# Additions and subtractions of two tensors from GpSimd to VectorE, clamps from VectorE to GpSimd, tail shifts to ScalarE

## Chip, cores and metric

The kernel runs on one core of a Trainium2 chip. The metric is the device time of one execution in microseconds (us). Before the change the median of 3 runs is 882.42 us (882.37 to 883.85).

## What is computed

Three layers follow one another, all in float32 (four batches of 576 tokens, 512 features):

```python
# 1. attention: 32 global queries see all keys, 512 local queries the global keys and a band of +-32
s_l = where(|i - j| <= 32, q_l @ k_l.T, -1e9);  a_l = softmax([q_l @ k_g.T, s_l]);  out = a_l @ v_all
# 2. dense MLP with a convolution over tokens as gate (w_in 512x1024, w_out 1024x512)
h = relu(x @ w_in);  conv = sum_k conv_w[k] * shift(h, k - 1);  x = (h * sigmoid(conv)) @ w_out
# 3. Fourier mixing, layer norm, dense MLP (w_ch1 512x2048, w_ch2 2048x512)
u = x + real(fft_features(fft_tokens(x)));  un = (u - mean(u)) / sqrt(var(u) + 1e-6)
out = u + relu(un @ w_ch1) @ w_ch2
```

The weights of layers 2 and 3 arrive as float64 (two 32-bit words a value), and the kernel itself makes float32 of them.

## The kernel before

**Weights.** There are 48 weight tiles of 128 x 512 values: 8 of `w_in` and 8 of `w_out` (`make_w`, L427), 16 of `w_ch1` and 16 of `w_ch2` (`make_c`, L698, and `make_cs`, L713). Each is loaded as 128 x 1024 words and goes through `unpack` and `from_f64` (L161 to L175): ScalarE takes the absolute value of the upper words, scaled by 2^16 (L163); a clamp to [2, TOP] follows (L164); the lower words are shifted right by 29 bits (the "tail shift", on VectorE in L168 or on ScalarE in L166); VectorE shifts the clamped value left by 3 and ors the tail in (L170), and then puts in the sign (L175). With `sign_act` the sign is made by ScalarE (L172) and multiplied in by GpSimd (L173) instead. `make_w` has the clamp on VectorE for `w_in` and on GpSimd for `w_out`; `make_c` and `make_cs` have it on VectorE always, the tail shift on VectorE for tiles 0 to 15 and on ScalarE for 16 to 31, and `sign_act` for every third tile (11 of 32).

**Two halves.** TensorE multiplies float32r operands in three passes (`mm3`, L144): high times high, and high times low twice. So each operand is split into a high part (ScalarE copy) and a low part, the difference of value and high part. For weights that is `put` (L201): ScalarE copy L203, GpSimd subtraction L204 (L718 and L719 in `make_cs`). `w_out` gets one step more, in `make_w`: sum and difference of its two halves (L433 on VectorE, L434 on GpSimd).

**Buffers for the unpacked value.** The `mag` tiles rotate: two of them up to tile 11 of layer 3, then three pieces of `misc`. A tile's chain holds one from L163 to the subtraction.

**Order of the work.** 32 attention steps (half a pair of heads each) run first; the first eight of them also unpack two tiles of layer 2 each. The units of layer 2 start in step 9 and run beside the rest of attention. Then come, interleaved, the end of layer 2, four Fourier transforms (`fft`, L616: sums and differences of mirrored tokens L623 to L629, two rounds of matmuls, and the results `ut` in L677 and L678), the 32 tiles of layer 3, and the first layer norm (`ln(0)`, L724). Layer 3's MLP is 8 chunks of 16 units: `c_g1` multiplies by `ch1`, L779 and L780 make relu and its low part, `c_g2` accumulates over `ch2`. Chunk 0 needs all 32 tiles; after it, `ln(c)` and L801 are the only work on GpSimd.

The queues of SP (loads) and TensorE follow the program's order throughout the attention part. All other orders are set ahead of time by a planner that simulates the engines with its own costs and takes, for each engine, the ready instruction of highest priority; on the chip each engine then works through its list in order. A change of costs or of engines thus changes the lists too. The weight loads of layer 2 are held back by the softmax of the step that asks for them (`anchor`).

The lines that matter most:

```python
(clamp or dve).tensor_scalar(mag, mag, 2.0, TOP, op0=ALU.max, op1=ALU.min)                       # L164
dve.scalar_tensor_tensor(val, val, 3, tail, op0=ALU.logical_shift_left, op1=ALU.bitwise_or)      # L170
gp.tensor_sub(t[:, 1], val, f32(t[:, 0]))                                                        # L204
```

Of the kernel before, what the change touches and what calls it, by code (L numbers as in the profile page):

```python
# [15 lines left out]
TOP = float(np.array([0x4FEFFFFF], np.uint32).view(np.float32)[0])  # L16
AF = mybir.ActivationFunctionType
ALU = mybir.AluOpType
# [4 lines left out]
S = SL + SG  # L23
# [5 lines left out]
NF = 274  # L29
# [95 lines left out]
def fused_kernel(ctx: ExitStack, tc: tile.TileContext, d, out):  # L125
    nc = tc.nc
    pe, act, dve, gp, sp = nc.tensor, nc.scalar, nc.vector, nc.gpsimd, nc.sync
# [27 lines left out]
    def f32(ap):  # L155
        return ap.bitcast(F32)
# [1 line left out]
    def bits(ap):  # L158
        return ap.bitcast(I32)

    def from_f64(raw, mag, clamp=None, tail_act=False, sign_act=False):  # L161
        head, tail = raw[:, :, 1], raw[:, :, 0]
        act.activation(mag, f32(head), AF.Abs, scale=65536.0)  # L163
        (clamp or dve).tensor_scalar(mag, mag, 2.0, TOP, op0=ALU.max, op1=ALU.min)  # L164
        if tail_act:
            act.activation(tail, tail.bitcast(U32), AF.Copy, scale=0.999 * 2.0**-29, bias=-0.499)  # L166
        else:
            dve.tensor_scalar(tail, tail, 29, None, op0=ALU.logical_shift_right)  # L168
        val = bits(mag)
        dve.scalar_tensor_tensor(val, val, 3, tail, op0=ALU.logical_shift_left, op1=ALU.bitwise_or)  # L170
        if sign_act:
            act.activation(f32(head), f32(head), AF.Sign)  # L172
            gp.tensor_mul(mag, mag, f32(head))  # L173
        else:
            dve.scalar_tensor_tensor(val, head, -(2**31), val, op0=ALU.bitwise_and, op1=ALU.bitwise_or)  # L175

    def fetch(pool, tag, src, after=None):
        t = pool.tile([128, 1024], I32, tag=tag, name="raw_" + tag)
# [13 lines left out]
    def unpack(pool, t, *how):  # L192
        if mags:
            mag = mags.pop(0)
            mags.append(mag)
        else:
            mag = pool.tile([128, 512], F32, tag="mag", name="mag", bufs=2)
        from_f64(t.rearrange("p (c b) -> p c b", b=2), mag, *how)
        return mag

    def put(pool, tag, val):  # L201
        t = pool.tile([128, 2, 512], F32R, tag=tag, name="w_" + tag)
        act.copy(t[:, 0], val)  # L203
        gp.tensor_sub(t[:, 1], val, f32(t[:, 0]))  # L204
        return t

    def rows_of(w, m):
# [19 lines left out]
    mp = left.enter_context(tc.tile_pool(name="mp", bufs=2))  # L227
# [192 lines left out]
    w_raw, w_in, w_out = {}, {}, {}  # L420
# [4 lines left out]

    @prio("w")
    def make_w(i):  # L427
        val = unpack(mp, w_raw.pop(i), gp if i >= 8 else dve)
        if i < 8:
            w_in[i] = put(wp, f"w{i}", val)  # L430
            return
        eo = mp.tile([128, 512], F32, tag="mag", name="mag", bufs=2)
        dve.tensor_add(eo[:, 0:256], val[:, 0:256], val[:, 256:512])  # L433
        gp.tensor_sub(eo[:, 256:512], val[:, 0:256], val[:, 256:512])  # L434
        w_out[i - 8] = put(wp, f"w{i}", eo)

    g_t, acc = {}, {}
# [178 lines left out]
    def fft(b):  # L616
        eo = eo_t[b]
        ff = fp.tile([128, 1024], F32, tag="v24", name="ff")
        fe = fd = ff[:, 0:2 * NF].rearrange("p (c n) -> p c n", c=2)
        fh = fp.tile([128, 4, NF], F32R, tag="v22", name="fh")  # L620
        fl = fp.tile([128, 4, NF], F32R, tag="v23", name="fl")
        rev = slice(S, S - NF, -1)
        gp.tensor_add(fe, eo[:, 0:2, 0:NF], eo[:, 0:2, rev])  # L623
        act.copy(fh[:, 0:2], fe)
        gp.tensor_sub(fl[:, 0:2], fe, f32(fh[:, 0:2]))
        gp.tensor_sub(fd, eo[:, 2:4, 0:NF], eo[:, 2:4, rev])
        dve.tensor_add(fd[0:1, 0], eo[0:1, 2, 0:NF], eo[0:1, 2, rev])
        act.copy(fh[:, 2:4], fd)
        gp.tensor_sub(fl[:, 2:4], fd, f32(fh[:, 2:4]))  # L629
        yield  # L630
        ab = fp.tile([128, 3084], F32R, tag="v29", name="ab")
        ah, al = [ab[0:92, 774 * i:774 * i + 774].rearrange("p (t k) -> p t k", t=3) for i in range(2)]
        bh, bl = [ab[0:92, 1548 + 768 * i:2316 + 768 * i].rearrange("p (t k) -> p t k", t=3) for i in range(2)]
        for t, (n0, nn) in enumerate(MT):
            ns = slice(n0, n0 + nn)
            o = fbank()[0:nn, 0:258]
            for c in range(2):
                mm3(o, fh[:, c, ns], fl[:, c, ns], c2[:, c, 0], c2[:, c, 1], c == 0, False)
            mm(o, fl[0:1, 2, ns], co, False, False)
            mm(o, fh[0:1, 2, ns], co, False, True)  # L640
            with pri("fev"):
                act.copy(ah[0:nn, t], o)
                dve.tensor_sub(al[0:nn, t], o, f32(ah[0:nn, t]))
            yield
            o = fbank()[0:nn, 0:256]
            for c in range(2):
                mm3(o, fh[:, 2 + c, ns], fl[:, 2 + c, ns], s2[:, c, 0], s2[:, c, 1], c == 0, c == 1)
            with pri("fev"):
                act.copy(bh[0:nn, t], o)
                dve.tensor_sub(bl[0:nn, t], o, f32(bh[0:nn, t]))  # L650
            yield
        if b not in u_t:
            u_t[b] = up.tile([128, 4, 546], F32, tag="u", name="u") if b else u0
        ut = u_t[b]
        back = slice(S - 1, HS, -1)
        for c in range(2):
            fs = slice(128 * c, 128 * c + 128)
            o = fbank()[:, 0:NF]
            for t, (n0, nn) in enumerate(MT):
                mm3(o, ah[0:nn, t, fs], al[0:nn, t, fs], c1[0:nn, t, 0], c1[0:nn, t, 1], t == 0, t == 2)  # L660
            e = eo[:, c]
            with pri("fev"):
                dve.scalar_tensor_tensor(
                    e[:, 0:HS + 1], e[:, 0:HS + 1], 0.5, o[:, 0:HS + 1], op0=ALU.mult, op1=ALU.add
                )
                dve.scalar_tensor_tensor(e[:, back], e[:, back], 0.5, o[:, 1:HS], op0=ALU.mult, op1=ALU.add)
            yield
            o = fbank()[:, 0:NF]
            for t, (n0, nn) in enumerate(MT):
                mm3(o, bh[0:nn, t, fs], bl[0:nn, t, fs], s1[0:nn, t, 0], s1[0:nn, t, 1], t == 0, t == 2)  # L670
            q = eo[:, 2 + c]
            with pri("fev"):
                dve.scalar_tensor_tensor(
                    q[:, 0:HS + 1], q[:, 0:HS + 1], 0.5, o[:, 0:HS + 1], op0=ALU.mult, op1=ALU.subtract
                )
                dve.scalar_tensor_tensor(q[:, back], q[:, back], 0.5, o[:, 1:HS], op0=ALU.mult, op1=ALU.add)
            dve.tensor_add(ut[:, c, 0:S], e[:, 0:S], q[:, 0:S])  # L677
            gp.tensor_sub(ut[:, 2 + c, 0:S], e[:, 0:S], q[:, 0:S])  # L678
            yield
        o = fbank()[0:1, 0:NF]  # L680
        for t, (n0, nn) in enumerate(MT):
            mm3(o, ah[0:nn, t, 256:257], al[0:nn, t, 256:257], c1[0:nn, t, 0], c1[0:nn, t, 1], t == 0, t == 2)
        r = ut[0:1, 2]
        dve.tensor_add(r[:, 0:HS + 1], r[:, 0:HS + 1], o[:, 0:HS + 1])
        dve.tensor_add(r[:, back], r[:, back], o[:, 1:HS])
        yield
# [3 lines left out]
    def c_slot(i):  # L690
        return (wp, f"w{i}") if i < 16 else (lw if i < 20 else fp, f"v{i}")
# [4 lines left out]

    @prio("cv")
    def make_c(i):  # L698
        t = put(*c_slot(i), unpack(mp, w_raw.pop(i), dve, i > 15, i % 3 == 0))
        if i < 16:  # L700
            ch1[i] = t
        else:
            ch2[i - 16] = t
# [8 lines left out]
    @prio("cv")  # L712
    def make_cs(i, k):  # L713
        raw = w_raw.pop(i)
        vals = [unpack(mp, raw[:, j], dve, True, (i + j) % 3 == 0) for j in range(k)]
        t = fp.tile([128, k, 2, 512], F32R, tag=f"v{i}", name="ws")
        for j in range(k):
            act.copy(t[:, j, 0], vals[j])  # L718
            gp.tensor_sub(t[:, j, 1], vals[j], f32(t[:, j, 0]))  # L719
            ch2[i + j - 16] = t[:, j]  # L720

    ln_t, dead = {}, {}
# [1 line left out]
    def ln(c):  # L724
        b, half = divmod(c, 2)
        ut = u_t[b][:, :, HS * half:HS * half + HS]
        scr = dead[min(c, 1)].rearrange("p a c -> p (a c)")
        cf = scr[:, 0:4 * HS].rearrange("p (a c) -> p a c", a=4)
        s4 = scr[:, 4 * HS:6 * HS].rearrange("p (a c) -> p a c", a=2)
        chl = xp.tile([128, 2, 4, HS], F32R, tag="xh", name="chl")  # L730
        ch, cl = chl[:, 0], chl[:, 1]
        sr = hdt[:, 3]
        gp.tensor_add(s4, ut[:, 0:2], ut[:, 2:4])
        gp.tensor_add(s4[:, 0], s4[:, 0], s4[:, 1])
        act.copy(sr[:, 0], s4[:, 0])
        dve.tensor_sub(sr[:, 1], s4[:, 0], f32(sr[:, 0]))  # L736
        yield
# [3 lines left out]
        mm(mu, ones, sr[:, 0], False, True)  # L741
        dve.tensor_sub(cf, ut, mu[:, None, :].to_broadcast([128, 4, HS]))  # L742
        act.copy(ch, cf)
        gp.tensor_sub(cl, cf, f32(ch))
        ln_t[c] = (ch, cl)
        yield
        act.activation(cf, cf, AF.Square)
        yield
        gp.tensor_add(s4, cf[:, 0:2], cf[:, 2:4])
        gp.tensor_add(s4[:, 0], s4[:, 0], s4[:, 1])  # L750
        yield
        act.copy(sr[:, 0], s4[:, 0])
        dve.tensor_sub(sr[:, 1], s4[:, 0], f32(sr[:, 0]))
# [172 lines left out]
```

## Time and profile before

| | |
|---|---|
| median of 3 runs | 882.42 us |
| the profiled execution | 884.08 us, of it span 881.9 us |
| TensorE matmul busy | 803.3 us (91%) |
| VectorE (DVE) busy | 505.4 us (57%) |
| ScalarE (ACT) busy | 347.4 us (39%) |
| GpSimd (POOL) busy | 308.6 us (35%) |
| mean granted TensorE clock | 0.94 of full speed |
| DMA | 48.33 MB, mean 55 GB/s |

Shares over the whole span say little here, as the stages differ. The span falls into: attention with the unpacking of layer 2's tiles (0 to 110 us), attention beside layer 2 (110 to 330), the change from layer 2 to layer 3 with transforms, tiles and first layer norm (330 to 550), and the MLP of layer 3 (550 to the end). Times in the trace are us from the span's start.

### The profile page before, as it was taken

How to read it: one execution, taken by the hardware profiler on the slowest of the kernel's cores; microseconds unless marked ns; L12 is line 12 of the kernel's file. 1: busy time of each engine (PE TensorE's matmuls, PEld its weight loads, DVE VectorE, ACT ScalarE, POOL GpSimd, SP SyncE). 2: the span in 40 equal slices, each digit the busy share in tenths (PEclk: the TensorE clock that was granted, in tenths of full speed). 3: DMA queues.
4: the chain of work that ended last, by engine and by line, in shares of the span. 5: the costliest groups of instructions: out<-in, count | busy, mean ns of one | idle time of the engine just before them, and what ended most of it. 6: DMA issues, size and time to landing. Idle time of an engine off the chain costs nothing. (4 is left out here: it accounts for less than half of the span.)

```text
span 881.9 us, 16202 instructions
## 1 busy us (share of the span) xinstructions
PE 803.3 (91%) x6436; PEld 752.0 (85%) x6436; DVE 505.4 (57%) x1222; ACT 347.4 (39%) x884; POOL 308.6 (35%) x318
## 2 busy tenths in 40 slices
PE   5767999999999999987779489999999999999997
PEld 3445788999899899877678388999999999999997
DVE  5786977686778767899788973221222222222212
ACT  4555555555555534555446552112121212121110
POOL 4878622132222222564676656022130404030100
PEclk8776999999999999989779699999999999999999
DMA  9460111101010012253304300000000000000000
GB/s 315 139 205 15 72 34 53 60 29 58 30 59 29 2 40 66 72 165 99 143 0 159 129 1 26 1 26 1 14 14 1 26 1 27 1 26 1 27 1 25
DMA packets 25387, 48.33 MB, mean 55 GB/s; under 512 B 1960, under 2 KB 18728, under 8 KB 25312
## 3 DMA queue, kind: packets, MB, share of 16 engines
q1 hardware_dynamic: 24480, 44.66, 15.0%
q0 software_dynamic: 832, 2.65, 1.2%
q8 instruction: 50, 0.82, 0.4%
q14 instruction: 25, 0.20, 0.1%
HBM read 43.23 MB, written 4.46 MB: 54 GB/s over the span
## 5 line engine op out<-in xcount | busy, mean ns | idle before, releaser
L302 POOL TENSOR_SCALAR pb<-pb,sm 128x224 f32<-128x224 f32 x128 | 72.9, 585 | 153.0 <-DVE sm L297 107.0
L142 PE MATMUL ps_a<-hdt,w_v 128*128 128x272 f32 x864 | 122.1, 290 | 0.0
L142 PE MATMUL ps_a<-g,w_w 128*128 128x272 f32 x768 | 114.1, 295 | 6.2 <-ACT g L486 4.4
L142 PE MATMUL ps_g<-xh,w_w 128*128 128x274 f32 x512 | 115.0, 303 | 0.0
L142 PEld LDWEIGHTS ps_a<-hdt,w_v 128*128 128x128 f32 x864 | 114.6, 191 | 0.0
L142 PE MATMUL ps_pv<-chl,w_w 128*128 128x272 f32 x768 | 109.7, 291 | 4.0 <-DVE hdt L780 3.8
L142 PE MATMUL ps_g<-chl,w_w 128*128 128x272 f32 x768 | 109.1, 290 | 2.4 <-DVE hdt L780 2.4
L142 PEld LDWEIGHTS ps_a<-g,w_w 128*128 128x128 f32 x768 | 103.2, 192 | 8.0 <-ACT g L486 5.2
L142 PEld LDWEIGHTS ps_pv<-chl,w_w 128*128 128x128 f32 x768 | 102.1, 191 | 5.3 <-issue 4.1
L142 PEld LDWEIGHTS ps_g<-chl,w_w 128*128 128x128 f32 x768 | 101.8, 190 | 3.1 <-DVE hdt L780 3.1
L780 DVE SCALAR_TENSOR_TENSOR hdt<-ps_pv,hdt 128x272 fp32r<-128x272 f32 x64 | 28.2, 440 | 122.0 <-ACT hdt L779 121.9
L142 PE MATMUL ps_a<-hdt,ws 128*128 128x272 f32 x672 | 92.5, 287 | 1.7 <-POOL ws L719 1.7
L801 POOL TENSOR_TENSOR misc<-misc,u 128x272 f32<-128x272 f32 x28 | 19.3, 720 | 212.6 <-DVE misc L800 212.6
L142 PEld LDWEIGHTS ps_g<-xh,w_w 128*128 128x128 f32 x512 | 86.7, 193 | 7.7 <-issue 4.4
L780 DVE SCALAR_TENSOR_TENSOR hdt<-ps_g,hdt 128x272 fp32r<-128x272 f32 x64 | 28.0, 437 | 109.2 <-ACT hdt L779 109.2
L142 PEld LDWEIGHTS ps_a<-hdt,ws 128*128 128x128 f32 x672 | 87.2, 188 | 1.9 <-POOL ws L719 1.9
L779 ACT ACTIVATE hdt<-ps_g 128x272 fp32r<-128x272 f32 x64 | 25.4, 397 | 128.1 <-PE ps_g L142 125.5
L779 ACT ACTIVATE hdt<-ps_pv 128x272 fp32r<-128x272 f32 x64 | 25.3, 395 | 128.0 <-PE ps_pv L142 127.1
L142 PE MATMUL ps_g<-xl,w_w 128*128 128x274 f32 x256 | 75.2, 294 | 0.0
L291 ACT ACTIVATE pb<-pb,sm 128x224 f32<-128x224 f32 x128 | 60.2, 472 | 15.6 <-DVE sm L279 15.6
L474 ACT ACTIVATE y<-y 128x272 f32<-128x272 f32 x64 | 27.5, 430 | 76.2 <-DVE y L468 76.2
L142 PE MATMUL ps_s<-qk 64*128 64x224 f32 (+1 forms) x144 | 40.1, 431 | 16.4 <-DVE smg L373 9.3
(211 smaller groups left out, 1489.4 us busy)
## 6 DMA issues: line engine op xcount, KB each, us to landing
qk<-in_qk_dram SPq DMA_DIRECT2D x16, 592.0 KB, 5.6
raw_w<-in_ch_dram SPq DMA_DIRECT2D x16, 512.0 KB, 3.8
v<-in_v_dram SPq DMA_DIRECT2D x8, 640.0 KB, 4.8
raw_v<-in_ch_dram SPq DMA_DIRECT2D x9, 512.0 KB, 5.8
out_dram<-misc SPq DMA_DIRECT2D x32, 136.0 KB, 1.8
raw_w<-in_w_in_dram SPq DMA_DIRECT2D x8, 512.0 KB, 5.1
raw_w<-in_w_out_dram SPq DMA_DIRECT2D x8, 512.0 KB, 4.0
raws<-in_ch_dram SPq DMA_DIRECT2D x7, 512.0 KB, 5.1
```

The source lines that it names most:

```text
L142: return pe.matmul(o, a, b, start=start, stop=stop)
L291: act.activation(p, p, AF.Exp, bias=sm[:, k:k + 1], scale=-1.0, accum_out=sm[:, 4 + k:5 + k])
L302: gp.tensor_scalar(p, p, sm[:, k:k + 1], 1.0, op0=ALU.mult, op1=ALU.mult)
L474: act.activation(g_t[u], g_t[u], AF.Tanh, scale=0.5)
L779: act.activation(hd[:, 0], o, AF.Relu)
L780: dve.scalar_tensor_tensor(hd[:, 1], o, 0.0, f32(hd[:, 0]), op0=ALU.max, op1=ALU.subtract)
L801: (dve if c == 7 else gp).tensor_add(o, o, u_t[b][:, e, HS * half:HS * half + HS])
```

## The change

The clamp goes to GpSimd for all 48 tiles (8 before), and its two operations change places (minimum first, then maximum). The tail shift goes to ScalarE for 8 of the 16 tiles of layer 2 (even numbers) and for all 32 of layer 3 (16 before). `sign_act` is gone, so that all signs are put in by VectorE (L175). The subtraction of `put` and of `make_cs`, the difference L434, the sums and differences of the transforms (L623, L625, L626, L629, L678) and, in the first layer norm only, its sums and the low part (L733, L734, L744, L749, L750) go from GpSimd to VectorE. The later layer norms and L801 stay on GpSimd.

```diff
-    def from_f64(raw, mag, clamp=None, tail_act=False, sign_act=False):
+    def from_f64(raw, mag, clamp=None, tail_act=False):
...
-        (clamp or dve).tensor_scalar(mag, mag, 2.0, TOP, op0=ALU.max, op1=ALU.min)
+        (clamp or dve).tensor_scalar(mag, mag, TOP, 2.0, op0=ALU.min, op1=ALU.max)
...
-        if sign_act:
-            act.activation(f32(head), f32(head), AF.Sign)
-            gp.tensor_mul(mag, mag, f32(head))
-        else:
-            dve.scalar_tensor_tensor(val, head, -(2**31), val, op0=ALU.bitwise_and, op1=ALU.bitwise_or)
+        dve.scalar_tensor_tensor(val, head, -(2**31), val, op0=ALU.bitwise_and, op1=ALU.bitwise_or)
...
     def put(pool, tag, val):
-        gp.tensor_sub(t[:, 1], val, f32(t[:, 0]))
+        dve.tensor_sub(t[:, 1], val, f32(t[:, 0]))
...
     def make_w(i):
-        val = unpack(mp, w_raw.pop(i), gp if i >= 8 else dve)
+        val = unpack(mp, w_raw.pop(i), gp, i % 2 == 0)
...
-        gp.tensor_sub(eo[:, 256:512], val[:, 0:256], val[:, 256:512])
+        dve.tensor_sub(eo[:, 256:512], val[:, 0:256], val[:, 256:512])
...
     def fft(b):
-        gp.tensor_add(fe, eo[:, 0:2, 0:NF], eo[:, 0:2, rev])
+        dve.tensor_add(fe, eo[:, 0:2, 0:NF], eo[:, 0:2, rev])
         act.copy(fh[:, 0:2], fe)
-        gp.tensor_sub(fl[:, 0:2], fe, f32(fh[:, 0:2]))
-        gp.tensor_sub(fd, eo[:, 2:4, 0:NF], eo[:, 2:4, rev])
+        dve.tensor_sub(fl[:, 0:2], fe, f32(fh[:, 0:2]))
+        dve.tensor_sub(fd, eo[:, 2:4, 0:NF], eo[:, 2:4, rev])
...
-        gp.tensor_sub(fl[:, 2:4], fd, f32(fh[:, 2:4]))
+        dve.tensor_sub(fl[:, 2:4], fd, f32(fh[:, 2:4]))
...
-            gp.tensor_sub(ut[:, 2 + c, 0:S], e[:, 0:S], q[:, 0:S])
+            dve.tensor_sub(ut[:, 2 + c, 0:S], e[:, 0:S], q[:, 0:S])
...
     def make_c(i):
-        t = put(*c_slot(i), unpack(mp, w_raw.pop(i), dve, i > 15, i % 3 == 0))
+        t = put(*c_slot(i), unpack(mp, w_raw.pop(i), gp, True))
...
     def make_cs(i, k):
-        vals = [unpack(mp, raw[:, j], dve, True, (i + j) % 3 == 0) for j in range(k)]
+        vals = [unpack(mp, raw[:, j], gp, True) for j in range(k)]
...
-            gp.tensor_sub(t[:, j, 1], vals[j], f32(t[:, j, 0]))
+            dve.tensor_sub(t[:, j, 1], vals[j], f32(t[:, j, 0]))
...
     def ln(c):
-        gp.tensor_add(s4, ut[:, 0:2], ut[:, 2:4])
-        gp.tensor_add(s4[:, 0], s4[:, 0], s4[:, 1])
+        eng = gp if c else dve
+        eng.tensor_add(s4, ut[:, 0:2], ut[:, 2:4])
+        eng.tensor_add(s4[:, 0], s4[:, 0], s4[:, 1])
...
-        gp.tensor_sub(cl, cf, f32(ch))
+        eng.tensor_sub(cl, cf, f32(ch))
...
-        gp.tensor_add(s4, cf[:, 0:2], cf[:, 2:4])
-        gp.tensor_add(s4[:, 0], s4[:, 0], s4[:, 1])
+        eng.tensor_add(s4, cf[:, 0:2], cf[:, 2:4])
+        eng.tensor_add(s4[:, 0], s4[:, 0], s4[:, 1])
```

## Rows read from the trace of the kernel before

**Rows 1.** Stages: length; busy us of PE, PEld, DVE, ACT, POOL; clock, DMA, GB/s.

```profile
0.00:110.00 110.00, 78.03 (x566) 58.68 (x566) 82.06 (x262) 58.36 (x164) 77.58 (x90) 0.78 0.45 149
110.00:330.00 220.00, 218.33 (x2039) 200.49 (x2036) 165.07 (x517) 119.19 (x362) 52.94 (x95) 0.99 0.12 38
...
366.00:531.00 165.00, 127.74 (x824) 115.45 (x822) 146.93 (x222) 88.14 (x173) 102.95 (x66) 0.84 0.30 99
...
550.00:882.00 332.00, 326.35 (x2610) 326.12 (x2608) 78.18 (x160) 59.03 (x133) 48.37 (x47) 1.00 0.04 13
```

**Rows 2.** Waits of TensorE in the whole span: us, times, longest.

```profile
PE ps_t L142 <- DVE hdt L736: 9.7, 2, 8.9
PE ps_s L142 <- DVE smg L373: 9.3, 2, 4.8
```

**Rows 3.** Groups of VectorE in 366:531: count, busy us, mean ns, idle before.

```profile
L164 DVE TENSOR_SCALAR misc<-misc 128x512 f32<-128x512 f32 x24 | 18.5, 772 | 5.8 <-ACT misc L163 5.8
L168 DVE TENSOR_SCALAR raw_w<-raw_w 128x512 int32<-128x512 int32 x16 | 10.7, 673 | 1.8 <-DMA raw_w<-in_ch_dram 1.8
...
L467 DVE SCALAR_TENSOR_TENSOR y<-h,convw,y 128x272 f32<-128x272 f32 x7 | 8.4, 1205 | 0.0
L170 DVE SCALAR_TENSOR_TENSOR misc<-misc,raw_w 128x512 int32<-128x512 int32 x8 | 8.3, 1041 | 0.1
L677 DVE TENSOR_TENSOR u<-u 128x544 f32<-128x544 f32 x7 | 8.3, 1188 | 0.0
L175 DVE SCALAR_TENSOR_TENSOR misc<-raw_v,misc 128x512 int32<-128x512 int32 x6 | 7.8, 1304 | 0.1
L170 DVE SCALAR_TENSOR_TENSOR misc<-misc,raws 128x512 int32<-128x512 int32 x7 | 7.4, 1065 | 0.4 <-ACT raws L166 0.3
L164 DVE TENSOR_SCALAR mag<-mag 128x512 f32<-128x512 f32 x8 | 6.5, 810 | 0.0
L175 DVE SCALAR_TENSOR_TENSOR misc<-raws,misc 128x512 int32<-128x512 int32 x5 | 6.2, 1239 | 0.0
```

**Rows 4.** VectorE in order of time: start, us, line (its unhindered durations).

```profile
403.00 0.68 DVE L170 SCALAR_TENSOR_TENSOR mag<-mag,raw_w 128x512 int32<-128x512 int32 x1
403.61 0.43 DVE L753 TENSOR_TENSOR hdt<-u,hdt 128x272 fp32r<-128x272 f32 x1
403.96 0.41 DVE L164 TENSOR_SCALAR misc<-misc 128x512 f32<-128x512 f32 x1
...
429.29 0.71 DVE L677 TENSOR_TENSOR u<-u 128x544 f32<-128x544 f32 x1
```

**Rows 5.** A clamp on GpSimd beside VectorE, then a subtraction beside it.

```profile
15.09 0.42 DVE L168 TENSOR_SCALAR raw_w<-raw_w 128x512 int32<-128x512 int32 x1
15.10 2.18 POOL L164 TENSOR_SCALAR mag<-mag 128x512 f32<-128x512 f32 x1 [1.89 <-ACT mag L163]
15.42 0.58 DVE L164 TENSOR_SCALAR cmag<-cmag 128x24 f32<-128x24 f32 x1
15.92 0.68 DVE L175 SCALAR_TENSOR_TENSOR mag<-raw_w,mag 128x512 int32<-128x512 int32 x1
...
84.70 1.70 POOL L204 TENSOR_TENSOR w_w<-mag,w_w 128x512 fp32r<-128x512 f32 x1
85.30 1.65 DVE L175 SCALAR_TENSOR_TENSOR mag<-raw_w,mag 128x512 int32<-128x512 int32 x1
```

**Rows 6.** Two lines on GpSimd, in the whole span: ns shortest/median/longest.

```profile
L164 POOL TENSOR_SCALAR mag<-mag x8: 1913/1915/2462, 15.1 to 101.1; 128x512 f32<-128x512 f32 x8
L386 POOL TENSOR_SCALAR sg<-sg,smg x8: 767/772/1273, 38.9 to 310.7; 128x608 f32<-128x608 f32 x8
```

**Rows 7.** Groups of GpSimd and VectorE in 0:110, columns as in Rows 3.

```profile
L204 POOL TENSOR_TENSOR w_w<-mag,w_w 128x512 fp32r<-128x512 f32 x15 | 21.0, 1402 | 4.2 <-issue 2.7 <-ACT w_w L203 1.3
...
L434 POOL TENSOR_TENSOR mag<-mag 128x256 f32<-128x256 f32 x8 | 6.6, 826 | 6.3 <-DVE sm L296 3.8 <-DVE sm L297 1.6 <-DVE mag L175 0.7
...
L170 DVE SCALAR_TENSOR_TENSOR mag<-mag,raw_w 128x512 int32<-128x512 int32 x16 | 11.9, 743 | 3.2 <-POOL mag L164 3.0
```

## The prediction

> **What bounds the kernel now.** Read the table of stages first [rows 1]. From 550 us on TensorE is busy for 326 of 332 us at full clock, and from 110 to 330 for 218 of 220: there no other engine sets the time, and what the change does there (little; from 550 nothing) is hidden. Two stages are open. In 0:110 TensorE is busy for 78 us, VectorE for 82, GpSimd for 78, and the granted clock is 0.78. In 366:531, where the transforms and the 32 tiles of layer 3 are made, TensorE is busy for 128 of 165 us and VectorE for 147: that stage is VectorE's, nearly without a gap. TensorE's longest waits, read next, say the same: they end with VectorE instructions [rows 2].
>
> Then ask why VectorE is busy, by its groups in 366:531 [rows 3] against the same instructions unhindered [rows 4]. A clamp of 128x512 (L164) takes 0.41 us when nothing is in its way, but 0.77 and 0.81 in the mean of the two groups; L170 and L175 take 0.68, but 1.04, 1.07, 1.24 and 1.30. The cause is to be seen in [rows 5]: the subtraction on GpSimd runs from 84.70 to 86.40, and an L175 that starts at 85.30 takes 1.65 us; it ends just after GpSimd does. So the two-tensor instructions on GpSimd hold VectorE up. Summed over the nine groups shown (mean less unhindered, times count; L168 as L164, the 272-wide L467 as L753, the 544-wide L677 by its own row): 8.7 + 4.2 + 5.4 + 2.9 + 3.3 + 3.7 + 2.7 + 3.2 + 2.8 = 36.9 us. These groups hold 82 of VectorE's 147 us; of the other 65, in narrower pieces, I count a sixth as stretched, 10 us (an estimate). Some 47 of 147 us are thus waiting and not work.
>
> **The change in 366:531.** *VectorE's own work grows.* It gets 29 weight subtractions (three of the 32 start after 531) and, with the sign of every third tile, 11 more L175: 40 x 0.68 = 27.2 us (L170, which also reads two tensors, in [rows 4]). It gets 7 additions and subtractions of the transforms and 7 of L678, 548 and 544 wide: 14 x 0.71 = 9.9. The first layer norm gives it two 544-wide and two 272-wide sums and one 1088-wide difference: 2 x 0.71 + 2 x 0.43 + 2 x 0.71 = 3.7. It loses 32 clamps and 16 tail shifts: 48 x 0.41 = 19.7. Net +21.1 us.
>
> *The stretching goes.* The subtractions, sign products and sums that caused it leave GpSimd, except for the second layer norm, for which I leave 4 us: -43. In their place come 32 clamps on GpSimd. What one of these does to VectorE shows in [rows 5]: during the clamp of 15.10 to 17.28 a tail shift takes 0.42 and an L175 0.68, unhindered both; only the 24-wide L164 right after the clamp's start is long, 0.58. Between 0 and 0.58 us a clamp, 0 to 18.6 in all, I take 0.2 (most of the neighbours are unhindered), +6.4. VectorE's sum: 21.1 - 43 + 6.4 = -15.5.
>
> *A new wait comes.* On GpSimd a clamp takes 1.91 us [rows 6] where VectorE took 0.41, and L170 waits for it at the head of VectorE's list, with all that stands behind it (evictions that TensorE waits for). In 0:110 eight clamps are on GpSimd already, and VectorE stood idle before L170 for 3.0 us on their account [rows 7]: 0.38 each, 12 us for 32. Against it, the 5.8 us that VectorE waited for L163 ahead of its own clamps [rows 3] are gone: +6. The bounds are 0 and 32 x 1.5 = 48. GpSimd itself has room: 32 x 1.91 = 61 us and the second layer norm, where it had 103. ScalarE gets 16 shifts and loses 11 signs, with 88 of 165 us busy; hidden as long as VectorE is the later one. So this stage: -15.5 + 6 = -9.5. The bounds are -28 (47 less the 4 left, less 21, and the 5.8 of waits) and +33 (-15.5 + 48).
>
> *Which order of the two operations?* L164 has minimum and maximum exchanged. The trace has only the old order on GpSimd, 1.91 us; another pair of operations on one tensor, L386, takes 0.77 for 608 columns [rows 6]. The new order may lie anywhere between, or above. I take 1.91, the same two operations.
>
> **The change in 0:110.** GpSimd loses 16 subtractions of 1.40 and eight L434 of 0.83, 29.0 us, and gets eight clamps more, 15.3: -13.7 of 78. VectorE gets 16 x 0.68 + 8 x 0.43 and loses eight clamps and eight shifts, 16 x 0.41: +7.8, less the stretching that goes there too (for L170, 0.743 against 0.68, 1 us). No engine is full, so neither number is the time. Softmax's L302 stands in GpSimd's list behind those subtractions, and TensorE's transposes behind L302; that queue gets shorter, while VectorE's gets longer. Between -13.7 and +7.8 I take -5, nearer to GpSimd's. ScalarE's eight shifts lie in its idle half (58 of 110 us busy).
>
> **The sum.** -9.5 - 5 = -14.5 on the profiled execution's 884.08 us (span 881.9 and 2.2 around it): 869.6. The median of the runs is 1.7 us lower, so in its terms 867.9; I say 868. The planner will order every list anew, and a wait such as the 8.9 us before L736 [rows 2] can come or go by that: +-9.
>
> **Two rules weighed.** *How long a clamp blocks.* Rows 5 have a subtraction that blocks to its end and a clamp that blocks for a fraction. The Trainium skill (SBUF — State Buffer, "Who interferes with whom") says that a GpSimd instruction and a VectorE instruction with two inputs in SBUF exclude each other for the whole instruction. By that rule the trace agrees for subtractions, but not for clamps; taken at its word it gives the second rival below. *What a clamp costs.* Rows 6 have 1.91 us for one tensor in. The Trainium skill (GPSIMD Engine Reference, "4.1 Engine selection") says that GpSimd is about two times slower with two inputs, and nearly at line rate with one. L386 agrees, the old clamp does not; if the new order does, it is the third rival.
>
> **Rivals.**
> 1. *VectorE waits in line for the clamps* (slower). L170 stands at the head of VectorE's list for 1.0 us a clamp rather than 0.38, for all 40 new clamps: 40 against the 12 counted, +28, so +13.5: 884.08 + 13.5 - 1.7 = 896. It decides from 0.38 + 14.5 / 40 = 0.74 us a clamp. For it: the clamp is 1.5 us longer than on VectorE, and two or three buffers for the value limit how far the planner can put other work between. Against it: GpSimd's queue gets shorter, and the one row on it shows 0.38. Chance 0.16.
> 2. *A clamp blocks VectorE to its end* (slower). Stretching came at 47 us for 103 of GpSimd; 71 us (61 and about 10 of the second layer norm) bring 32, not the 10.4 counted: +22, so +7: 890. Against it [rows 5]. Chance 0.08.
> 3. *The new order of operations is fast on GpSimd*, about 0.7 us as L386. The new waits fall from 12 to 4, and in 0:110 GpSimd loses a further 16 x 1.2 = 19 us, for which I give 5: -14.5 - 8 - 5 = -27.5: 855. Chance 0.17.
> 4. *Something else holds 366:531*: the loads of the last tiles, or the second layer norm, whose sums stay on GpSimd ahead of L736 (the 8.9 us of [rows 2]). Of the 14.5 us little remains: 878 to 882. For it: VectorE is idle for 18 of the 165 us. Chance 0.15, a third of it within 0.2%.
>
> The forecast itself (859 to 877) has 0.44. About 0.2%, 1.8 us, is what a measurement of this kernel can tell from no change. Faster: 0.44 + 0.17 + 0.10 = 0.71. Same: 0.05. Slower: 0.24. The range 848 to 887 takes in the forecast, rivals 3 and 4 and the nearer part of 1; the likeliest case's own is 859 to 877.
>
> **What would show it.** In the profile after: L170 and L175 at 0.7 us in the mean and L204 at about 0.7 on VectorE; VectorE's busy time in the stage of the tiles down to some 130 us, and that stage to about 155; the stage ahead of layer 2 about 5 us shorter; 550 to the end unchanged at 332. L164 on GpSimd at 1.91 or near 0.7 tells the forecast from rival 3; idle time before L170 put down to L164 of over 0.7 us a clamp would make rival 1 right and the prediction wrong, and stretched L170 beside clamps would make rival 2 right.

## The result and the profile after

| | before | after |
|---|---|---|
| median | 882.39 us (879.97 to 883.85) | 853.30 us (851.66 to 855.29) |
| ratio, 95% interval | | 0.9674 (0.9642 to 0.9706) |
| profiled execution / its span | 884.08 / 881.9 us | 851.66 / 849.9 us |
| TensorE matmul busy / idle in the span | 803.3 / 78.6 us | 785.3 / 64.6 us |
| VectorE, ScalarE, GpSimd busy | 505.4, 347.4, 308.6 us | 486.2, 353.8, 197.4 us |
| mean granted clock | 0.94 | 0.965 |

The change takes 29.1 us off; 14.5 were forecast. It is faster, inside the range (848 to 887), but below the forecast's own band (859 to 877): near rival 3, which had 855. All medians here are of undisturbed executions: one of the four executions of the change with all clamps on VectorE (second batch) took 2597 us and is left out, and with it the only profile of that kernel.

The kernel after is four lines shorter from L173 on (three later): L204 of before is L200, L175 is L171, L719 is L715, L736 is L733.

To see where the time went, both spans are cut at the same two events: the first copy of layer 2's output out of PSUM (L515 before, L511 after), and the point from which the last 342 us are the same work. Columns as in [rows 1]. Before, first and middle stage:

```profile
0.00:140.07 140.07, 106.43 (x820) 85.20 (x821) 104.84 (x332) 75.57 (x217) 86.07 (x104) 0.82 0.38 127
140.07:539.90 399.83, 360.43 (x2930) 330.56 (x2929) 319.41 (x724) 210.81 (x531) 167.27 (x160) 0.94 0.20 64
```

After, the same two stages, and the last 342 us:

```profile
0.00:128.03 128.03, 99.35 (x820) 79.09 (x821) 101.43 (x339) 79.63 (x225) 53.75 (x88) 0.89 0.41 139
128.03:507.90 379.87, 349.45 (x2930) 322.41 (x2929) 303.66 (x748) 213.93 (x537) 90.31 (x122) 0.96 0.21 68
...
508.00:850.00 342.00, 336.35 (x2689) 336.13 (x2687) 80.99 (x168) 60.22 (x136) 53.21 (x53) 1.00 0.04 14
```

The first stage is 12.0 us shorter, the middle 20.0, the end not at all (the same 336.35 us of TensorE in 342 before). Compare TensorE's column with the stage's length: the matmuls are the same in number (820 and 2930), yet their own time fell by 7.1 and 11.0 us, with the granted clock up from 0.82 to 0.89 and from 0.94 to 0.96. TensorE's idle time (length less busy) fell by 4.9 us (33.6 to 28.7) and 9.0 (39.4 to 30.4). So in these two executions 14 of the 32 us of the span are waits that went, and 18 are matmuls that ran faster. The prediction had no term for the second.

This split is that of two executions which lie far apart. The mean clock was 0.938 to 0.954 in 28 executions of the kernel before (0.946 in their mean; this one 0.94) and 0.955 to 0.965 in eight of the change (0.960; this one 0.965). The traces show only two levels, 2.4 GHz and half of it, so the time at the lower one is twice the missing share: 105 and 60 us in these two executions, 46 apart, but 96 and 68 in the mean of all, 28 apart. Of the 29.1 us between the medians the faster matmuls are thus nearer to 11 than to 18 (an estimate, 18 x 28 / 46).

VectorE's groups in the last stretch of the middle (343.5 to 508, the tiles of layer 3), columns as in [rows 3], which they answer:

```profile
L171 DVE SCALAR_TENSOR_TENSOR misc<-raw_v,misc 128x512 int32<-128x512 int32 x9 | 9.3, 1042 | 0.0
L200 DVE TENSOR_TENSOR w_v<-misc,w_v 128x512 fp32r<-128x512 f32 x9 | 7.5, 832 | 0.4 <-ACT w_v L199 0.2
L715 DVE TENSOR_TENSOR ws<-misc,ws 128x512 fp32r<-128x512 f32 x7 | 6.2, 918 | 1.5 <-ACT ws L714 1.5
L673 DVE TENSOR_TENSOR u<-u 128x544 f32<-128x544 f32 x8 | 6.2, 772 | 0.0
L170 DVE SCALAR_TENSOR_TENSOR misc<-misc,raw_v 128x512 int32<-128x512 int32 x9 | 6.1, 690 | 1.4 <-POOL misc L164 1.4
L171 DVE SCALAR_TENSOR_TENSOR misc<-raws,misc 128x512 int32<-128x512 int32 x7 | 6.1, 868 | 0.1
L170 DVE SCALAR_TENSOR_TENSOR misc<-misc,raws 128x512 int32<-128x512 int32 x7 | 5.9, 848 | 0.6 <-POOL misc L164 0.6
...
L170 DVE SCALAR_TENSOR_TENSOR misc<-misc,raw_w 128x512 int32<-128x512 int32 x8 | 5.4, 678 | 0.0
```

Read the mean in ns: L170 is at 678 to 848 (953 to 1065 before, the 953 in a group that [rows 3] leaves out), L673 at 772 (1188 as L677 before). The new subtractions (L200, L715) take 832 and 918 in the last 16 tiles, some of them beside the later layer norms on GpSimd. The stretching of these groups, mean less unhindered as in the prediction, is 3.3 + 1.4 + 1.7 + 0.5 + 0.1 + 1.3 + 1.2 = 9.5 us (the 678 is unhindered), where nine groups of before had 36.9.

The clamp on GpSimd in the whole span (ns shortest/median/longest), and who waited for it (us, times), answering [rows 6] and [rows 7]:

```profile
L164 POOL TENSOR_SCALAR mag<-mag x24: 607/614/3340, 13.2 to 395.8; 128x512 f32<-128x512 f32 x24
L164 POOL TENSOR_SCALAR misc<-misc x24: 610/628/1290, 384.3 to 496.1; 128x512 f32<-128x512 f32 x24
...
  DVE misc L170: 1.9, 2
...
  DVE mag L170: 0.5, 1
```

With minimum first and maximum second it takes 0.61 us, not 1.91, and VectorE waits 2.4 us for all 48.

TensorE's longest waits, columns as in [rows 2]:

```profile
PE ps_t L142 <- DVE hdt L733: 9.4, 2, 8.7
PE ps_a L142 <- DVE w_v L200: 7.7, 1, 7.7
...
PE ps_s L142 <- DVE smg L369: 5.3, 1, 5.3
```

The 8.9 us before L736 are still there (L733, 8.7). The second wait is for a weight's low part, now VectorE's.

### The profile page after: what moved, and what is told of

It is laid out like the page before. It is cut to its first block, busy times and chain, and to the rows that moved or that the text cites. A ratio compares the mean times of both kernels' runs of the same rounds, so it can differ in the third digit from the quotient of the medians.

```text
span 849.9 us, 16132 instructions
## 1 busy us (share of the span) xinstructions
PE 785.3 (92%) x6436; PEld 737.7 (87%) x6436; DVE 486.2 (57%) x1254; ACT 353.8 (42%) x897; POOL 197.4 (23%) x262
## 3 DMA queue, kind: packets, MB, share of 16 engines
q1 hardware_dynamic: 24480, 44.66, 15.5%
## 4 chain that ended last, share of the span: by engine, by line
PE 75%; DVE 11%; DMA 7%; ACT 3%; issue 2%; POOL 1%; SPq 0%; DVEq 0%; ACTq 0%; POOLq 0%
PE ps_a L142 31%; PE ps_g L142 21%; PE ps_pv L142 13%; PE ps_s L142 5%; PE ps_t L142 2%; DMA raw_w<-in_ch_dram 2%; DMA raw_v<-in_ch_dram 1%; DMA raw_w<-in_w_out_dram 1%; DMA raw_w<-in_w_in_dram 1%; DMA co<-in_co_dram 1%; DVE w_w L200 1%; DVE mag L171 1%; DVE mag L170 1%; DVE pb L275 1%; DVE misc L170 1%
## 5 line engine op out<-in xcount | busy, mean ns | idle before, releaser
L142 PE MATMUL ps_a<-g,w_w 128*128 128x272 f32 x768 | 111.1, 291 | 1.4 <-DVE g L483 0.8
L142 PE MATMUL ps_pv<-chl,w_w 128*128 128x272 f32 x768 | 106.7, 288 | 0.2 <-DVE hdt L777 0.2
L142 PEld LDWEIGHTS ps_a<-g,w_w 128*128 128x128 f32 x768 | 100.8, 188 | 2.6 <-DVE g L483 1.2
L142 PEld LDWEIGHTS ps_pv<-chl,w_w 128*128 128x128 f32 x768 | 100.2, 188 | 0.6 <-DVE hdt L777 0.4
L798 POOL TENSOR_TENSOR misc<-misc,u 128x272 f32<-128x272 f32 x28 | 19.5, 728 | 216.4 <-DVE misc L797 216.4
```

What stands on the lines that cost most here:

```text
L142: return pe.matmul(o, a, b, start=start, stop=stop)
L798: (dve if c == 7 else gp).tensor_add(o, o, u_t[b][:, e, HS * half:HS * half + HS])
```

## The experiments

All ratios are against the kernel before, timed in the same batch (881.42, 882.38 and 881.98 us); intervals are 95%. "Idle" is TensorE's: the profiled span less its matmul busy time.

### First batch: which part carries it

Theory 1: it pays that two-tensor work leaves GpSimd, and what a clamp costs is hidden. Theory 2: the fast clamp makes half of the gain.

**The change with the old order of operations in the clamp.**

```diff
-        (clamp or dve).tensor_scalar(mag, mag, TOP, 2.0, op0=ALU.min, op1=ALU.max)
+        (clamp or dve).tensor_scalar(mag, mag, 2.0, TOP, op0=ALU.max, op1=ALU.min)
```

> The changed kernel with the clamp's two operations in the order of the kernel before (maximum, then minimum) on all engines; nothing else. The changed kernel's median is 853.3 us, and its clamp on GpSimd takes 0.61 us. Theory 1 (what counts is that two-tensor work has left GpSimd; GpSimd has room, so the price of a clamp is hidden): the clamp is back at 1.91 us, the time within 3 us of 853. Theory 2 (the fast clamp made the gain twice the forecast, rival 3 of the prediction): VectorE stands idle before L170 for about 0.4 us a clamp, and the time is the forecast's, 865 to 870. If the order has no influence at all on the clamp (it is fast for another reason), the clamp stays at 0.61 and the time at 853.

Measured: 863.28 us, 0.9805 (0.9776 to 0.9833), between the two and nearer to Theory 2. L164 in this kernel:

```profile
L164 POOL TENSOR_SCALAR mag<-mag x24: 1908/1918/4647, 13.0 to 400.1; 128x512 f32<-128x512 f32 x24
L164 POOL TENSOR_SCALAR misc<-misc x24: 1909/2156/2527, 389.0 to 507.4; 128x512 f32<-128x512 f32 x24
...
  DVE misc L170: 5.7, 5
  DVE mag L170: 5.1, 5
```

The operands, the engine and the shape are the same: the order alone makes 1.91 us of 0.61. VectorE waits 10.8 us for 48 such clamps, 0.225 each (the prediction had 0.38, from a single wait of 3.0 us in eight clamps). The order is worth 10.0 us here. This is the kernel that the forecast priced: 18.1 us less than before, where 14.5 were forecast.

In the two traces, of this kernel and of the change, all five engines work through the same instructions in the same order. So these 10 us come from the clamp's duration alone, not from other lists. Little of it is waiting: TensorE's idle time is 66.1 us here and 64.6 in the change, its matmul time 794.1 and 785.3 (64.9 and 782.6 in the change once more, below). Over all executions the mean clock is 0.954 here and 0.960 in the change, 79 and 68 us at the lower level, so in the mean some 7 of the 8.8 us stay (an estimate, scaled as above).

**The kernel before with the new order alone** (eight clamps on GpSimd).

```diff
-        (clamp or dve).tensor_scalar(mag, mag, 2.0, TOP, op0=ALU.max, op1=ALU.min)
+        (clamp or dve).tensor_scalar(mag, mag, TOP, 2.0, op0=ALU.min, op1=ALU.max)
```

> The kernel before with the clamp's operations in the new order (minimum, then maximum); its eight clamps on GpSimd stay there, the others on VectorE. Theory 1: GpSimd loses 8 x 1.3 = 10 us ahead of 110 us, a queue that TensorE's transposes wait for only in part: 878 to 882. Theory 2 (the slow clamp is what holds the first stage): 873 to 877. Clamps on VectorE stay at 0.41 us unhindered under both.

Measured: 878.85 us, 0.9972 (0.9949 to 0.9995), 2.6 us: Theory 1's band, for eight clamps. On GpSimd the median clamp goes from 1915 to 614 ns; on VectorE the order makes no difference (414 and 416 ns, the 24 clamps of `misc`).

**The kernel before with the weights' subtractions on VectorE.**

```diff
-        gp.tensor_sub(t[:, 1], val, f32(t[:, 0]))
+        dve.tensor_sub(t[:, 1], val, f32(t[:, 0]))
...
-        gp.tensor_sub(eo[:, 256:512], val[:, 0:256], val[:, 256:512])
+        dve.tensor_sub(eo[:, 256:512], val[:, 0:256], val[:, 256:512])
...
-            gp.tensor_sub(t[:, j, 1], vals[j], f32(t[:, j, 0]))
+            dve.tensor_sub(t[:, j, 1], vals[j], f32(t[:, j, 0]))
```

> The kernel before with the weights' subtractions alone (L204, L719 and the difference L434) on VectorE; clamps, tail shifts, signs, transforms and layer norm as before. Theory 1: VectorE gets 29 x 0.68 = 20 us in the stage of the 32 tiles and loses the stretching that these subtractions caused there, some 25 to 30 us; in the first stage GpSimd loses 28 us: 868 to 874, about half of the whole gain. Theory 2: VectorE is merely loaded with more work and, with the clamps still on it, ends later: 880 to 888.

Measured: 866.25 us, 0.9835 (0.9808 to 0.9861), 15.2 us: better than Theory 1 had. Three edits of one word each are half of the gain. Both stages in this kernel:

```profile
0.00:133.40 133.40, 103.10 (x820) 82.06 (x821) 108.19 (x355) 75.34 (x217) 60.61 (x80) 0.87 0.39 133
133.40:522.50 389.10, 357.17 (x2930) 326.62 (x2929) 320.36 (x756) 211.74 (x532) 135.29 (x130) 0.96 0.20 66
```

VectorE's middle is as full as before (320.4 for 319.4 us), so it got 32 subtractions for the price of the stretching they had caused; TensorE's idle went from 39.4 to 31.9.

**The change with those subtractions back on GpSimd.**

```diff
-        dve.tensor_sub(t[:, 1], val, f32(t[:, 0]))
+        gp.tensor_sub(t[:, 1], val, f32(t[:, 0]))
...
-            dve.tensor_sub(t[:, j, 1], vals[j], f32(t[:, j, 0]))
+            gp.tensor_sub(t[:, j, 1], vals[j], f32(t[:, j, 0]))
```

> The changed kernel with the weights' subtractions alone (put, make_cs and the difference of w_out's halves) back on GpSimd; clamps in the new order on GpSimd, shifts, signs, transforms and first layer norm as in the changed kernel. Theory 1: GpSimd's 48 subtractions of 1.3 us and more stretch VectorE again, and GpSimd carries 0.61 + 1.35 us a tile: 868 to 878. Theory 2 (the fast clamps and the work taken off VectorE make the gain): 850 to 858, since VectorE loses 48 x 0.68 us.

Measured: 861.94 us, 0.9775 (0.9735 to 0.9816): without them the change still has 19.5 us, between the theories. The subtractions alone give 15.2 us and the rest without them 19.5, together more than the whole: the two gains overlap.

### Second batch: the other parts

Each expectation weighs two theories of its own, A and B.

**The change with all clamps on VectorE.**

```diff
-        val = unpack(mp, w_raw.pop(i), gp, i % 2 == 0)
+        val = unpack(mp, w_raw.pop(i), dve, i % 2 == 0)
...
-        t = put(*c_slot(i), unpack(mp, w_raw.pop(i), gp, True))
+        t = put(*c_slot(i), unpack(mp, w_raw.pop(i), dve, True))
...
-        vals = [unpack(mp, raw[:, j], gp, True) for j in range(k)]
+        vals = [unpack(mp, raw[:, j], dve, True) for j in range(k)]
```

> The changed kernel with all clamps on VectorE; the rest as in the changed kernel. VectorE gets 32 x 0.41 = 13 us more in the stage of the tiles and 16 x 0.41 = 6.6 in the first, and no clamp on GpSimd stretches it or keeps it waiting. Theory A (VectorE's work and stretching set that stage, and a fast clamp on GpSimd costs VectorE next to nothing): 862 to 868, 9 to 15 us over the changed kernel, about as bad as the slow clamp on GpSimd (863.3). Theory B (a clamp on either engine is as good, since VectorE loses stretching and waits of the same size): 852 to 857.

Measured: 863.57 us (three executions), 0.9809 (0.9763 to 0.9855): as A had it, 10.3 us over the change. Without the clamps' move, all the rest of the change gives about what the subtractions alone give (866.25; the intervals overlap).

**The kernel before with all clamps on GpSimd, in the new order** (L164 as above).

```diff
-        val = unpack(mp, w_raw.pop(i), gp if i >= 8 else dve)
+        val = unpack(mp, w_raw.pop(i), gp)
...
-        t = put(*c_slot(i), unpack(mp, w_raw.pop(i), dve, i > 15, i % 3 == 0))
+        t = put(*c_slot(i), unpack(mp, w_raw.pop(i), gp, i > 15, i % 3 == 0))
...
-        vals = [unpack(mp, raw[:, j], dve, True, (i + j) % 3 == 0) for j in range(k)]
+        vals = [unpack(mp, raw[:, j], gp, True, (i + j) % 3 == 0) for j in range(k)]
```

> The kernel before with all clamps on GpSimd in the new order; subtractions, tail shifts, signs, transforms and layer norm as before. Theory A: VectorE loses 13 us of clamps (23 with their stretching) in the stage of the tiles, but GpSimd, with subtractions and sign products, gets 32 x 0.61 = 20 us onto its 103 and delays the chains: 870 to 876. Theory B (clamps and subtractions do not depend on each other): the whole difference that clamps on GpSimd make in the changed kernel, 866 to 870.

Measured: 890.88 us, 1.0102 (1.0054 to 1.015): slower by 8.5 us, which neither theory had. Its middle stage, and TensorE's longest waits:

```profile
135.90:548.50 412.60, 366.06 (x2931) 335.57 (x2931) 305.84 (x694) 210.73 (x531) 189.35 (x195) 0.92 0.19 62
```

```profile
PE ps_a L142 <- POOL w_v L204: 15.3, 2, 14.6
PE ps_a L142 <- POOL ws L719: 8.6, 3, 5.4
```

VectorE has 13.6 us less to do there than before, and the stage is 12.8 us longer. Added over all of TensorE's waits of the middle, those that end with a GpSimd instruction were 1.7 us before and are 27.2 here; those that end with VectorE fell from 32.3 to 17.2. GpSimd's list ahead of the 14.6 us wait shows what stands before the awaited subtraction (start, us, line):

```profile
486.08 2.91 POOL L204 TENSOR_TENSOR w_w<-misc,w_w 128x512 fp32r<-128x512 f32 x2 [1.92 <-ACT w_w L203]
488.95 1.27 POOL L173 TENSOR_TENSOR misc<-misc,raw_v 128x512 f32<-128x512 f32 x1
490.19 1.33 POOL L733 TENSOR_TENSOR u<-u 128x544 f32<-128x544 f32 x1
492.11 0.61 POOL L164 TENSOR_SCALAR misc<-misc 128x512 f32<-128x512 f32 x1 [0.59 <-ACT misc L163]
...
494.64 1.66 POOL L204 TENSOR_TENSOR w_v<-misc,w_v 128x512 fp32r<-128x512 f32 x1 [0.61 <-ACT w_v L203]
```

Clamps, sign products, subtractions and layer norm sums of several tiles share one list, which is busy for 72 of the 100 us from 400 to 500; its gaps here (0.6 to 1.9 us) end with ScalarE's instructions of the same chains. Each tile goes through the list two or three times, with VectorE in between. So a cheap clamp can be dear in a list that already holds the end of the same chain. That the list's length makes the 8.5 us is argued from these waits: all engines' lists differ from those of the kernel before.

**The change with the transforms' sums and the first layer norm back on GpSimd** (L619, L621, L622, L625 and L674 alike).

```diff
-        dve.tensor_add(fe, eo[:, 0:2, 0:NF], eo[:, 0:2, rev])
+        gp.tensor_add(fe, eo[:, 0:2, 0:NF], eo[:, 0:2, rev])
...
-        eng = gp if c else dve
+        eng = gp
```

> The changed kernel with the sums and differences of the transforms (L623 to L629, L678 of the kernel before) and those of the first layer norm back on GpSimd; weights as in the changed kernel. Theory A: 14 + 5 instructions of 0.7 us (13.6 us) leave VectorE and come back as stretching (GpSimd gets some 14 x 1.7 + 8 us): 857 to 862. Theory B (GpSimd is nearly empty, so these instructions are as well off there): 850 to 855.

Measured: 856.08 us, 0.9709 (0.9665 to 0.9753): 2.8 us more than the change, between A and B; the intervals overlap.

**The change with the second layer norm on VectorE too.**

```diff
-        eng = gp if c else dve
+        eng = gp if c > 1 else dve
```

> The changed kernel with the second layer norm's sums and low part on VectorE too (those of the third to eighth stay on GpSimd). In the changed kernel these stand on GpSimd at 456.1 to 460.5 (two sums, 3.3 and 1.1 us) while TensorE waits 8.7 us for L736's successor, and the low part at 465.3 stretches two L175 on VectorE to 3.98 us together. Theory A: both go: 847 to 851. Theory B (the wait is for the last transform's end, which this does not move, and VectorE has more to do): 852 to 855.

Measured: 850.16 us, 0.9647 (0.9611 to 0.9683): 3.1 us less than the change and in A's band, but the two intervals overlap.

### Third batch: do subtractions and clamps make the whole?

C has the two make nearly all of the change; D adds the two effects as measured alone (-15.2 and +8.5).

**The kernel before with the subtractions on VectorE and the fast clamps on GpSimd** (the whole diffs of those two experiments).

```diff
-        gp.tensor_sub(t[:, 1], val, f32(t[:, 0]))
+        dve.tensor_sub(t[:, 1], val, f32(t[:, 0]))
...
-        t = put(*c_slot(i), unpack(mp, w_raw.pop(i), dve, i > 15, i % 3 == 0))
+        t = put(*c_slot(i), unpack(mp, w_raw.pop(i), gp, i > 15, i % 3 == 0))
```

> The kernel before with two parts of the change only: the weights' subtractions on VectorE, and all clamps on GpSimd in the new order. Tail shifts, signs, transforms and layer norm are as before. By themselves the two gave -15.2 and +8.5 us. Theory C (the clamp pays only when GpSimd has been emptied: the two parts together make nearly the whole change): 853 to 858. Theory D (the parts add up, and the rest of the change, signs, shifts, transforms and first layer norm, makes the remaining 22 us): 873 to 877.

Measured: 863.89 us, 0.98 (0.9775 to 0.9824), neither C nor D. The clamps cost 8.5 us alone; once the subtractions have left GpSimd they cost nothing (2.4 us less, with intervals that overlap). The two effects do not add, as that would give 875. But 11 us of the change are still missing.

**The change with tail shifts and signs shared out as before** (the reverse of the diff's parts on `tail_act` and `sign_act`; the clamp stays on GpSimd).

```diff
+        if sign_act:
+            act.activation(f32(head), f32(head), AF.Sign)
+            gp.tensor_mul(mag, mag, f32(head))
...
-        t = put(*c_slot(i), unpack(mp, w_raw.pop(i), gp, True))
+        t = put(*c_slot(i), unpack(mp, w_raw.pop(i), gp, i > 15, i % 3 == 0))
```

> The changed kernel with tail shifts and signs divided as in the kernel before: shifts on VectorE for all 16 tiles of layer 2 and the first 16 of layer 3, every third sign of layer 3 by ScalarE and GpSimd. VectorE gets 24 x 0.41 = 10 us and loses 11 x 0.68 = 7.5; GpSimd gets 11 products of 1.3 us, which stretch VectorE. Theory C: 855 to 860. If shifts and signs make nothing: within 2 us of the changed kernel beside it.

Measured: 864.87 us, 0.9806 (0.9781 to 0.9831), above what C had. The shifts and signs, which all but cancel in the prediction's count of VectorE's work (16 x 0.41 us lost, 11 x 0.68 got), carry 12 us together; the two were not parted. Both stages:

```profile
0.00:131.20 131.20, 100.77 (x820) 81.05 (x821) 106.03 (x347) 75.16 (x217) 55.46 (x88) 0.88 0.40 135
131.20:522.70 391.50, 362.94 (x2932) 334.31 (x2931) 310.70 (x753) 213.09 (x532) 112.05 (x133) 0.92 0.21 66
```

Idle in the middle is 28.6 us, *less* than the change's 30.4. What is longer is the matmuls' own time: 362.9 for 349.5 us. This does not hang on one execution: the mean clock was 0.945 to 0.948 in all four of this kernel, against 0.955 to 0.965. Slices of 10 us show where. This kernel, from 410:

```profile
410.00:420.00 10.00, 7.98 (x35) 6.93 (x36) 10.00 (x22) 2.82 (x7) 0.00 (x0) 0.62 0.18 54
420.00:430.00 10.00, 9.44 (x40) 7.94 (x39) 3.38 (x9) 4.57 (x10) 0.89 (x2) 0.50 0.74 262
430.00:440.00 10.00, 8.72 (x37) 7.05 (x36) 10.00 (x18) 4.98 (x9) 4.20 (x4) 0.50 0.02 5
440.00:450.00 10.00, 8.85 (x35) 7.38 (x36) 9.82 (x18) 6.54 (x12) 6.47 (x4) 0.50 0.14 49
450.00:460.00 10.00, 10.00 (x79) 9.66 (x79) 9.25 (x15) 7.15 (x15) 5.84 (x5) 1.00 0.49 169
```

and the change in the same slices:

```profile
400.00:410.00 10.00, 6.85 (x44) 5.62 (x44) 10.00 (x22) 4.21 (x9) 0.00 (x0) 1.00 0.48 151
410.00:420.00 10.00, 7.47 (x31) 5.96 (x32) 5.59 (x11) 7.00 (x15) 1.84 (x3) 0.57 0.41 165
420.00:430.00 10.00, 10.00 (x73) 9.82 (x72) 9.99 (x19) 5.36 (x10) 2.78 (x3) 0.92 0.00 0
430.00:440.00 10.00, 9.46 (x70) 7.99 (x69) 10.00 (x21) 4.39 (x10) 1.83 (x2) 1.00 0.16 55
```

In both the clock falls in 410:420, after a slice in which TensorE was busy for 7 of 10 us. In the change it is back at the 2.4 GHz level early in 420:430, a slice in which TensorE has no gap; in the other kernel TensorE's gaps go on (9.44, 8.72, 8.85), and the clock stays at 0.50, the 1.2 GHz level, until 450. From 420 to 450 it does 112 matmuls in 27.0 us there, 0.241 each; the change does 143 in the 19.5 us from 420 to 440, 0.136 each. A busy column that is nearly full hides that. A full slice does not always bring the clock back: with subtractions and clamps alone, 420:430 is busy for 10.00 at 0.50 and only 430:440 is at 0.92. That gaps hold the clock down is thus a reading of these slices, and not shown.

**The change once more, as it is.**

> The changed kernel once more, as it is, on the chip of the runs beside it, as their yardstick: 851 to 856.

Measured: 852.67 us, 0.9671 (0.9634 to 0.9708), as in the first timing: the differences of 10 us and more between the kernels are not those between batches.

**The change with all four layer norms' sums on VectorE.**

```diff
-        eng = gp if c else dve
+        eng = dve
```

> The changed kernel with the sums and low parts of all layer norms on VectorE. The second layer norm alone gave 850.2 us, against 853.3. From 508 us on TensorE sets the time and VectorE is idle for three quarters, so the others should change nothing: 847 to 851, under the changed kernel beside it by about 3. If VectorE's larger share puts L780's low part of the hidden units late, TensorE waits in the last 342 us: 853 or more.

Measured: 847.42 us, 0.9605 (0.9579 to 0.963): faster than both kernels, by 5 us against the change. TensorE's longest waits:

```profile
PE ps_t L142 <- DVE hdt L733: 9.7, 2, 8.9
...
PE ps_a L142 <- DVE w_v L200: 3.3, 1, 3.3
```

The wait before L733 stays; the one for a weight's low part falls from 7.7 to 3.3 us. What led to the 7.7 us stands in the change's timeline, where the second layer norm is still GpSimd's (start, us, line, idle before):

```profile
465.33 2.92 POOL L741 TENSOR_TENSOR chl<-u,chl 128x1088 fp32r<-128x1088 f32 x1 [2.51 <-ACT chl L740]
465.84 3.98 DVE L171 SCALAR_TENSOR_TENSOR misc<-raw_v,misc 128x512 int32<-128x512 int32 x2
...
468.84 0.62 ACT L199 CAST w_v<-misc 128x512 fp32r<-128x512 f32 x1 [3.02 <-DVE misc L171]
469.74 0.68 DVE L200 TENSOR_TENSOR w_v<-misc,w_v 128x512 fp32r<-128x512 f32 x1
...
470.48 4.90 PE L142 MATMUL ps_a<-hdt,w_v 128*128 128x272 f32 x20 [7.68 <-DVE w_v L200]
```

Of the two L171, 0.68 us each when unhindered, the first takes 2.96 beside the wide subtraction on GpSimd and the second 1.09 beside a clamp, 3.98 together. ScalarE's high part of the first tile (L199) waits 3.02 us for the first; the low part (L200) starts at 469.74, when the second is done, and TensorE after it. By the profiled executions the gain is waiting that went: TensorE's idle time falls from 64.6 to 55.8 us, while its matmul time is 6.1 us longer.

### The kernels side by side

Us; span, busy and idle are those of the profiled execution, the clock is the mean over all executions of the kernel (28 of before, eight of after, four of each other).

| kernel | median | span | TensorE busy | idle | mean clock |
|---|---|---|---|---|---|
| before | 882.4 | 881.9 | 803.3 | 78.6 | 0.946 |
| before, all clamps on GpSimd | 890.9 | 890.5 | 805.1 | 85.4 | 0.944 |
| before, subtractions on VectorE | 866.3 | 864.5 | 796.7 | 67.8 | 0.957 |
| before, subtractions and clamps | 863.9 | 864.3 | 797.9 | 66.4 | 0.951 |
| after, old shifts and signs | 864.9 | 864.7 | 800.1 | 64.6 | 0.946 |
| after, old order in the clamp | 863.3 | 860.2 | 794.1 | 66.1 | 0.954 |
| after | 853.3 | 849.9 | 785.3 | 64.6 | 0.960 |
| after, all layer norms on VectorE | 847.4 | 847.2 | 791.4 | 55.8 | 0.962 |

Read the idle column first: the subtractions alone take 10.8 of the 14 us of idle time, and the four kernels from the fourth row to the seventh are within 1.8 us of each other. They differ in the column before it, by up to 14.8 us: the same 6436 matmuls at another clock. (Part of the 14.8 is the choice of execution: the medians of these two kernels are 11.6 apart.) That is the second part of the change's gain.

One experiment, the order in the clamp, holds every engine's list fixed, and there the matmul time moves by 8.8 us with the clamp's duration alone. In the other experiments the planner orders lists anew (only a little for the layer norms), so what an edit gives there is the move and the new order together; no run parts them. Why the clock's low stretches fall where they do stays open.

## Why the prediction was right in sign and half in size

- **What bounds the kernel.** Right: the two stages named gave all the time, and the last stretch none.
- **VectorE's sum, -15.5 us.** Right as a count: its busy time in the middle went from 319.4 to 303.7 us, -15.8 (the stage of the forecast lies in it); the stretching left over is 9.5 us where 10.4 was taken (4 + 6.4). Those 9.5 are of the groups shown alone. From the first tile's L163 to the end of the middle it fell from 148.8 to 131.5 us (the forecast had some 130). The durations behind it held for the most part: L170 at 0.68 to 0.85, L200 at 0.70 to 0.83, L715 at 0.92.
- **VectorE's busy time taken as the stage's time.** Wrong as a rule. With all clamps on GpSimd it fell by 13.6 us and the stage grew by 12.8; with the subtractions alone it rose by 1.0 and the stage lost 10.7. In the change itself the part from the first tile on lost 22.2 us (173.4 to 151.2) with VectorE's 17.3. What TensorE's longest waits point to instead is when a weight's low part is ready, through whichever list.
- **"I take 1.91, the same two operations."** This choice failed. The clamp takes 0.61 us; in the old order the change gains 18.1 us, inside the forecast's own band, in the new one 10.0 more.
- **The new wait, +6 (12 less 5.8).** Mis-sized: VectorE waits 2.4 us for all 48 clamps, and 10.8 even with the slow one (0.225 a clamp, not 0.38, which rested on one wait).
- **0:110, -5.** Mis-sized: the stage gave 12.0, of it 4.9 idle time and 7.1 of faster matmuls; with the slow clamp 7.1, nearly all of it idle time (6.6).
- **A term that was missing.** The sum counted waits alone. This is the step behind most of the miss. In the kernel that it priced, with the old order, TensorE's idle time fell by 12.5 us, for 14.5 forecast, and its matmul time by 9.2, which the sum put at nothing. In the change the idle time fell by 14.0, near the 14.5 partly by luck, as the clamp was not the one priced; the other 18 us of the span are matmul time in the profiled executions. This step and the one on the clamp's price overlap: of what the fast order gave, 8.8 us are matmul time. [rows 1] had shown the clock at 0.78 and 0.84 in just the two open stages.
- **Shifts and signs.** ScalarE's part was called hidden, and no run speaks against that; VectorE's came out near nothing (-6.6 and +7.5). Put back together, they cost 12 us, in matmul time and not in waits: what was missed is the same term.
- **Rival 1** fell: 0.05 us a clamp, 0.225 with the slow one, far below the 0.74 from which it decides.
- **Rival 2** fell: of VectorE's 128x512 two-tensor instructions on weights (L170, L171, L200, L715) the 81 with GpSimd idle beside them took 0.68 us in the mean, the 29 beside clamps alone 0.76 (median 0.68), the 34 beside other GpSimd work 0.96. The rule of the Trainium skill (SBUF — State Buffer, "Who interferes with whom") that it rests on is borne out here for two-tensor work on GpSimd (the 2.96 us above), but not for most clamps.
- **Rival 3** came true in its price and its time, 0.61 us for its 0.7 and 853.3 for its 855. Its gain had 13 us and got 10.0, but by another path, so that its time is partly luck: VectorE's waits for clamps fell by 8.4 us, as it had them (12 to 4), yet TensorE's idle time by 1.5 only, and 8.8 us came as matmul time. What the Trainium skill (GPSIMD Engine Reference, "4.1 Engine selection") says of one-input work holds here for one order of the two operations (0.61 us), not for the other (1.91).
- **Rival 4** fell: its wait before L736 did stay (8.7 us), and the gain came all the same; all layer norms on VectorE gave 5 us more, with that wait still there.

## What to carry to other kernels

Count TensorE's time as waits plus matmul time at the granted clock: where a stage shows a clock below full, an edit on another engine can move the second more than the first (8.8 and 1.5 us by the clamp's order, with all lists the same). Take the clock of several executions before splitting a gain so. Price work that is moved by the list it joins: the same clamps cost 8.5 us in a GpSimd list full of two-tensor work, and brought 10.3 in the changed kernel, where most of that had gone. Where one instruction has two operations, try both orders before it is priced.

## What was not expected of the hardware

- One instruction of GpSimd, 128x512 float32 in place, with a minimum and a maximum against constants: 1.91 us with the maximum first, 0.61 with the minimum first. On VectorE the order made no difference (0.41).
- The same 6436 matmuls took between 782.6 us (the change once more) and 805.1 us (all clamps on GpSimd, from before) in kernels that do the same arithmetic.
